# Sliding-window attention and a SMELU layer on one core: the first batch's q and k ahead of w_in, three SMELU slots on VectorE, and the last output tile in one piece

## The chip, the cores and the metric

The kernel runs on one core of a Trainium2 chip. The metric is the device time of one execution in microseconds. A profile, taken in one execution, shows what each engine did; its times count from the first instruction of its span.

## The reference

Eight batches with eight heads of 576 positions and 64 columns: attention in a window of 32 positions to each side, then a layer of 512 to 2048 to 512 columns with the SMELU function between its two products. All matrices come in float32, the output is float32.

```python
scores = scale * np.matmul(q, k.transpose(0, 1, 3, 2))
mask = np.abs(pos[:, None] - pos[None, :]) <= window        # window = 32
attn = softmax(np.where(mask, scores, -1e9))
x = (attn @ v).transpose(0, 2, 1, 3).reshape(4608, 512)
h = x @ w_in                                                # 512 x 2048
g = np.where(h >= 1, h, np.where(h <= -1, 0.0, (h + 1) ** 2 / 4))
out = g @ w_out                                             # 2048 x 512
```

## The kernel before

**Order.** All instructions stand in an order written out by hand; each engine runs its own in that order, and waits for what they read and for the buffers they write. A loop over `a` (line 483) runs through "slots". Slot a works on the 256 positions t = a // 8 and on 256 of the 2048 middle columns, f = a % 8. In a slot come: the products with w_in (eight matmuls, line 504, into the PSUM tile hp), SMELU, whose result goes to gT in bf16, then attention steps that the table `ev` puts there (`at(a, ...)`), then output products (`post`): the first four output tiles as "pairs" of 256 columns (function `pair`, line 460), all later ones as quarters of a tile (function `quarter`, line 444).

**SMELU.** ScalarE makes rr = relu(0.5 h + 0.5) (line 508). Then there are two ways: VectorE takes mx = max(h, rr) (line 515) and g = min(rr, 1) * mx (line 516); or, in the slots of the list `two_on_act`, ScalarE squares rr (line 512) and VectorE takes g = min(max(h, 1), rr²) (line 513). hp lies in a pool of two buffers (ps_h); slot 6 uses the pool ps_o.

**Attention.** For one batch, q and k are transposed on TensorE for batches 0 and 1 (`tpose`, line 187 and 189) and copied out of PSUM by ScalarE and VectorE (line 190); later batches are transposed by a DMA. `scores` adds a mask bias by matmul (line 206, early batches only), multiplies q and k (line 227) and takes exp on ScalarE (line 235); for later batches VectorE multiplies by a mask (line 201). `sums` multiplies by v and by ones (line 293) and has its quotient made as exp(-ln) on ScalarE (lines 299 and 300); VectorE's product with it is written to xT (lines 305 and 308), which is what slots read. `muls` and `flush` keep that last product back until VectorE's turn. The steps of `sums` and `scores` use the pools ps_s and ps_n, of one buffer each.

**Warm-up.** Ahead of slot 0, half of q and k of batch 0 is transposed and the first 256 positions of each pair of heads go through scores and sums. `keep_warm` puts matmuls without use in between (line 336). The other half (`qh`, `kh`, loaded by `load_half`, line 85) is transposed in slot 1, its scores follow in slots 2 and 3, its sums in slots 3 to 5.

**Loads.** All loads but q's first half are issued by GpSimd, with a cast to bf16, in the order of `put` (lines 144 to 157): v of batch 0, w_in for slots 0 and 1 (four loads of 128 KB, 64 rows of partitions each), the other half of q and k of batch 0 (four of 144 KB), w_in for slots 2 to 7 with w_out's first part among them, then three copies that build the masks (lines 151 and 153), w_out, and q, k and v of batch 1. Each load uses one of eight semaphores in turn, so each waits until the load eight places before it has landed. SyncE issues the stores and the DMA transposes.

**Tail.** The last output tile is made in two halves of 256 columns, and each is copied by ScalarE (line 437) and stored (line 438) by itself; a full tile is copied at line 449 and stored at line 450.

Of the kernel before, what the change touches and what calls it, by code (L numbers as in the profile page):

```python
# [7 lines left out]
FP = mybir.dt.float32  # L8
BF = mybir.dt.bfloat16
AF = mybir.ActivationFunctionType  # L10
ALU = mybir.AluOpType
# [3 lines left out]
def kernel(  # L15
# [19 lines left out]
    nc = tc.nc  # L35
# [106 lines left out]
    def put(todo):  # L142
        for fn, *x in todo:
            fn(*x)
# [1 line left out]
    w = [(load_w_in, c, c + 256, h) for c in range(0, 1024, 256) for h in range(2)]  # L146
    w += [(load_w_in, 1024, 1536, h) for h in range(2)]
    w += [(load_w_in, c, c + 256, h) for c in range(1536, DFF, 256) for h in range(2)]
    put(w[:4] + [(load_half, 1, t, h) for t in range(2) for h in range(2)] + w[4:12])
    put([(load_w_out, 0, 0, 4)] + w[12:])  # L150
    P.tensor_copy(band[HD[1], 0:128], band[HD[1], 64:192])
    for m, n, x in ((mask4, 8, 128), (mask8, 4, TAIL)):
        P.tensor_copy(m.rearrange("p (n j) -> p n j", n=n),
                      band[:, :x].rearrange("p (n j) -> p n j", n=1).to_broadcast([128, n, x]))
    put([(load_w_out, 0, 4, 8), (load_w_out, 0, 8, 16)] + [(load_rows, 1, t) for t in range(2)])
    put([(load_v, 1, n) for n in range(4)] + [(load_w_out, 1, 8 * n, 8 * n + 8) for n in range(2)])
    put([(load_nat, 2, t) for t in range(2)] + [(load_v, 2, n) for n in range(4)])

# [10 lines left out]
    def tpose(b, n, t, copy, ps):  # L169


        half, part = divmod(n, 2)
        j0, j1 = ((0, 5), (5, 9))[part]
        if b:
            src = qn[b] if t == 0 else kn[b]
            src = [src[:, half + 2 * h] for h in range(2)]
            dst = qkT(b, t).rearrange("d (y e p j) -> d y e p j", y=2, e=2, j=9)[:, half, :, :, j0:j1]
            like = "d j (e p) -> d e p j"
        else:
            src = (qn, kn)[t][b, half]  # L180
            src = src if src.shape[1] == 9 else [src[:, h] for h in range(2)]
            dst = qkT(b, t).rearrange("d (y l p j) -> d l y p j", l=2, p=32, j=9)[:, half, :, :, j0:j1]
            like = "d j (p y) -> d y p j"
        for j in range(j0, j1):
            if isinstance(src, list):
                for h in range(2):
                    nc.tensor.transpose(ps[HD[h], j - j0], src[h][:, D * j:D * j + D], ident)  # L187
            else:
                nc.tensor.transpose(ps[:, j - j0], src[:, j], ident)
        return lambda: copy(dst, ps[:, :j1 - j0].rearrange(like, p=64 if b else 32))  # L190
# [120 lines left out]
    def flush():  # L311
        while muls:
            muls.pop(0)()
# [18 lines left out]
    def keep_warm(n, pool, tag):  # L332

        z = pool.tile([128, 512], FP, name="z", tag=tag)
        for _ in range(n):
            nc.tensor.matmul(z, warm[:, :128], warm, start=True, stop=True)
# [9 lines left out]
    with tc.tile_pool(name="ps_p", bufs=1, space=bass.MemoryType.PSUM) as ps_p:  # L346
        keep_warm(11, ps_h, "hp")

        V.memset(qkT(0, 0).rearrange("d (y s) -> d y s", y=NY)[:, :, S // 2:352], 0.0)
        for b in range(LONG):  # L350
            V.memset(qkT(b, 0).rearrange("d (y s) -> d y s", y=NY)[:, :, S - PAD:], 0.0)
        V.memset(qkT(0, 1).rearrange("d (y s) -> d y s", y=NY)[:, :, S // 2:320], 0.0)
        qn[0, 0] = cast(q32, "qb", 5)
        qq = [tpose(0, n, 0, (A.copy, V.tensor_copy)[n], tp1(ps_h)) for n in range(2)]
        for x in qq:
            x()
        kk = [tpose(0, n, 1, (A.copy, V.tensor_copy)[n], tp1((ps_n, ps_p)[n])) for n in range(2)]
        keep_warm(3, ps_h, "hp")
        for x in kk:
            x()  # L360
        scores(0, (0, 1), (0, 2), (0, 2), None)
        scores(0, (0, 2), (0, 1), (2, 3), None, ps_n, 32)
        scores(0, (1, 2), (0, 2), (0, 2), None, ps_p)
        keep_warm(4, ps_h, "hp")
        e0 = sums(0, 0, 0, TB)
        keep_warm(2, ps_h, "hp")
        e1 = sums(0, 1, 0, TB, ps_p)
        keep_warm(7, ps_h, "hp")
        e0()
        e1()  # L370
    ps_o = ctx.enter_context(tc.tile_pool(name="ps_o", bufs=2, space=bass.MemoryType.PSUM))


# [1 line left out]

    NB = NT // TB
    NF = DFF // 256
    pairs = [(6, 0), (8, 1), (9, 2), (10, 3), (11, 4), (12, 5), (15, 6), (15, 8), (16, 7), (17, 9)]
    two_on_act = (1, 7, 8, 9, 10, 11, 12)
    ev = {}  # L380

    def at(a, *todo):


        ev.setdefault(a, []).extend(x for x in todo if x)
# [5 lines left out]
                yield (sums, b, y1, lo, hi), (scores, b, (y1, y1 + 1), (0, 2), (2 * k, 2 * k + 2))  # L391
        yield (sums, b, 0, MAIN, S), (scores8, b)

    at(1, (tposes, 0, (0, 1), (1, 1)))
    at(2, (scores, 0, (0, 1), (0, 2), (2, 4)), (scores8, 0, ps_o))
    at(3, (scores, 0, (1, 2), (0, 2), (2, 4), ps_n), (sums, 0, 0, TB, MAIN, ps_s))
    at(4, (sums, 0, 1, TB, MAIN))
    at(5, (sums, 0, 0, MAIN, S, ps_s))
    seq = [x for b in range(1, B) for x in steps(b, 224)]
    at(13, seq[0][1])  # L400
    at(13.5, (*seq[1][1], ps_n))
    at(14, (*seq[0][0], ps_s), seq[1][0])
    at(16, seq[2][1])
    for n, a in enumerate((18, 20, 26.5, 28)):
        at(a, seq[2 + n][0])
    for n, a in enumerate((18, 20, 26.5, 28)):
        at(a, seq[3 + n][1])
# [16 lines left out]
    def quarter(x):  # L424

        tt, ff = divmod(x, 4)
        if tt == NT // 128 - 1:
            half, n = divmod(ff, 2)
            if n == 0:
                op[tt] = ps_o.tile([128, 256], FP, name="op", tag="op")  # L430
            cols = slice(256 * half, 256 * half + 256)
            for j in range(NF * n, NF * n + NF):
                nc.tensor.matmul(op[tt], gT[tt // 2][:, j, 128 * (tt % 2):128 * (tt % 2) + 128], w_out[:, j, cols],  # L433
                                 start=j == 0, stop=j == 2 * NF - 1)
            if n:
                osb = osp.tile([128, 256], FP, name="osb")
                A.copy(osb, op[tt])
                nc.sync.dma_start(out=out[128 * tt:128 * tt + 128, cols], in_=osb)
            return
        if tt not in op:  # L440
            op[tt] = ps_o.tile([128, DM], FP, name="op", tag="op"), []
        o, done = op[tt]
        for j in range(4 * ff, 4 * ff + 4):
            nc.tensor.matmul(o, gT[tt // 2][:, j, 128 * (tt % 2):128 * (tt % 2) + 128], w_out[:, j],  # L444
                             start=not done, stop=len(done) == 2 * NF - 1, skip_group_check=True)
            done.append(j)
        if len(done) == 2 * NF:
            osb = osp.tile([128, DM], FP, name="osb")
            A.copy(osb, o)  # L449
            nc.sync.dma_start(out=out[128 * tt:128 * tt + 128, :], in_=osb)  # L450
# [31 lines left out]
    for a in range(NF * NB + NF):  # L482
        t, f = divmod(a, NF)
        eng = None if a < 14 else V
        post = [x for n, x in pairs if n == a] + [a - NF] * (a >= 2 * NF + 2)
        for b, x in loads.get(a, []):
            if x < 2:
                load_nat(b, x)
            else:
                for n in range(4):  # L490
                    load_v(b, n)
        if a == 0 or a > 3:
            flush()
        if t < NB:
            if t not in gT:
                gT[t] = gtp.tile([128, 2 * NF, TB], BF, name="gT", tag="gT")
            r0 = TB * t % RING
            if a == 6:
                hp = ps_o.tile([128, 2, TB], FP, name="hp", tag="op")
            else:  # L500
                hp = ps_h.tile([128, 2, TB], FP, name="hp", tag="hp")
            for j in range(2):
                for n, kk in enumerate((0, 2, 1, 3)):
                    nc.tensor.matmul(hp[:, j], w_in[:, kk, 256 * f + 128 * j:256 * f + 128 * j + 128],  # L504
                                     xT[:, kk, r0:r0 + TB], start=n == 0, stop=n == 3)

            rr = ewp.tile([128, 2, TB], FP, name="rr")
            A.activation(rr, hp, AF.Relu, scale=0.5, bias=0.5)  # L508
            g = gT[t][:, 2 * f:2 * f + 2]
            mx = ewp.tile([128, 2, TB], FP, name="mx")  # L510
            if a in two_on_act:
                A.activation(mx, rr, AF.Square)
                V.scalar_tensor_tensor(g, hp, 1.0, mx, op0=ALU.max, op1=ALU.min)
            else:
                V.tensor_max(mx, hp, rr)  # L515
                V.scalar_tensor_tensor(g, rr, 1.0, mx, op0=ALU.min, op1=ALU.mult)  # L516
        flush()
        run(a)
        for x in post:
            (pair if x < 4 * 4 else quarter)(x)  # L520
        run(a + 0.5)
        for x in xps.get(a, []):
            xpose(*x)
# [30 lines left out]
```

## Time and profile before

| | |
|---|---|
| median of 3 runs | 308.55 us (308.35 to 308.8) |
| the profiled execution's own time | 308.55 us |
| its span | 306.8 us |
| TensorE busy | 295.2 us, 96% of the span, 3613 matmuls |
| VectorE busy | 241.8 us, 79% |
| ScalarE busy | 192.3 us, 63% |
| GpSimd busy | 76.8 us, 25% |
| chain of waits, by engine | PE 88%, DMA 4%, issue 3%, ACT 2%, POOL 1%, DVE 1% |
| granted TensorE clock | 1.0 |

In the profile's lines PE is TensorE, PEld its weight loads, DVE VectorE, ACT ScalarE, POOL GpSimd, SP SyncE. L504 is line 504 of the kernel. A line of the timeline gives the start, the time, engine, line, operation, tiles and shape, the number of such operations, and in brackets the idle time of the engine before it and what ended it. The chain of waits is followed back from the last instruction: at each step to what released it.

### The profile page before, as it was taken

How to read it: one execution, taken by the hardware profiler on the slowest of the kernel's cores; microseconds unless marked ns; L12 is line 12 of the kernel's file. 1: busy time of each engine (PE TensorE's matmuls, PEld its weight loads, DVE VectorE, ACT ScalarE, POOL GpSimd, SP SyncE). 2: the span in 40 equal slices, each digit the busy share in tenths (PEclk: the TensorE clock that was granted, in tenths of full speed). 3: DMA queues.
4: the chain of work that ended last, by engine and by line, in shares of the span. 5: the costliest groups of instructions: out<-in, count | busy, mean ns of one | idle time of the engine just before them, and what ended most of it. 6: DMA issues, size and time to landing. Idle time of an engine off the chain costs nothing.

```text
span 306.8 us, 8458 instructions
## 1 busy us (share of the span) xinstructions
PE 295.2 (96%) x3613; PEld 206.8 (67%) x3650; DVE 241.8 (79%) x376; ACT 192.3 (63%) x320; POOL 76.8 (25%) x91
## 2 busy tenths in 40 slices
PE   8999999999999999999999999999999999999995
PEld 3567878876666666666666666666666666666654
DVE  4278568888888888889888888889888888888760
ACT  3688786738856667666656666566676666554431
POOL 8798451028008205500550002800000000000000
PEclk9999999999999999999999999999999999999999
DMA  9999999999999997996899155990811010010111
GB/s 150 182 196 197 179 201 151 175 153 151 133 208 82 171 164 124 155 114 141 103 168 140 34 112 105 142 158 17 178 49 36 34 36 36 35 36 34 61 44 68
DMA packets 137157, 35.70 MB, mean 116 GB/s; under 512 B 122144, under 2 KB 132896, under 8 KB 137120
## 3 DMA queue, kind: packets, MB, share of 16 engines
q0 software_dynamic: 102960, 18.06, 81.1%
q1 hardware_dynamic: 34016, 16.81, 25.6%
q8 instruction: 28, 0.46, 0.6%
q10 hardware_dynamic: 144, 0.29, 0.4%
q14 instruction: 9, 0.07, 0.1%
HBM read 36.70 MB, written 9.44 MB: 150 GB/s over the span
## 4 chain that ended last, share of the span: by engine, by line
PE 88%; DMA 4%; issue 3%; ACT 2%; POOL 1%; DVE 1%; POOLq 0%; ACTq 0%
PE hp L504 39%; PE op L444 34%; PE bb L293 6%; PE op L460 4%; PE bb L227 2%; DMA w_in<-in_moe_w_in_dram 2%; DMA vn<-in_v_dram 2%; PE op L433 1%; ACT pt L235 1%; PE tp L187 1%; POOL kh L85 1%; DVE xT L305 0%; DVE mx L515 0%; POOL vn L106 0%; PE bb L206 0%
## 5 line engine op out<-in xcount | busy, mean ns | idle before, releaser
L504 PE MATMUL hp<-xT,w_in 128*128 128x256 bf16 x1152 | 149.6, 273 | 1.4 <-DMA w_in<-in_moe_w_in_dram 0.6
L508 ACT ACTIVATE rr<-hp 128x512 f32<-128x512 f32 x144 | 85.6, 594 | 88.1 <-PE hp L504 88.1
L504 PEld LDWEIGHTS <-w_in 128*128 128x128 bf16 x1152 | 112.0, 98 | 41.1 <-issue 2.3
L444 PE MATMUL op<-w_out,gT 128*128 128x512 bf16 x461 | 119.6, 379 | 5.0 <-issue 4.8
L515 DVE TENSOR_TENSOR mx<-hp,rr 128x512 f32<-128x512 f32 x137 | 94.4, 689 | 30.9 <-ACT rr L508 28.9
L516 DVE SCALAR_TENSOR_TENSOR gT<-rr,mx 128x512 bf16<-128x512 f32 x137 | 95.2, 695 | 4.7
L444 PEld LDWEIGHTS <-gT 128*128 128x128 bf16 x496 | 46.1, 98 | 34.8
L98 POOL DMA_DIRECT2D qn<-in_q_dram x12 | 14.6, 1221 | 111.8 <-DMA kT<-kn 108.2
L235 ACT ACTIVATE pt<-bb 128x1024 bf16<-128x1024 f32 (+1 forms) x33 | 32.7, 1001 | 4.8 <-PE bb L227 3.4
L305 DVE TENSOR_TENSOR xT<-bb,rc 128x512 bf16<-128x512 f32 (+1 forms) x32 | 21.0, 657 | 10.1 <-ACT rc L300 9.5
L106 POOL DMA_DIRECT2D vn<-in_v_dram x32 | 27.5, 899 | 4.4 <-DMA w_out<-in_moe_w_out_dram 4.4
L300 ACT ACTIVATE rc<-lr 128x512 f32<-128x512 f32 (+2 forms) x40 | 23.5, 587 | 1.3
L449 ACT COPY osb<-op 128x512 f32<-128x512 f32 x31 | 18.0, 582 | 8.7 <-PE op L444 8.3
L299 ACT ACTIVATE lr<-bb 128x512 f32<-128x512 f32 (+2 forms) x40 | 22.1, 551 | 0.3 <-PE bb L293 0.3
L201 DVE TENSOR_TENSOR pt<-pt,mask 128x1024 bf16<-128x1024 bf16 (+1 forms) x33 | 20.2, 613 | 0.5 <-ACT pt L235 0.5
L293 PE MATMUL bb<-pt,ones 64*64 64x256 bf16 (+3 forms) x352 | 19.6, 256 | 0.1
L293 PE MATMUL bb<-pt,vn 64*64 64x128 bf16 (+3 forms) x712 | 18.4, 204 | 0.1
L293 PEld LDWEIGHTS <-vn 64*64 64x64 bf16 x712 | 16.7, 107 | 0.3 <-DMA vn<-in_v_dram 0.3
L460 PE MATMUL op<-w_out,gT 128*128 128x256 bf16 x128 | 16.5, 273 | 0.0
L293 PEld LDWEIGHTS <-ones 64*64 64x64 bf16 x352 | 10.2, 106 | 8.9 <-issue 8.9
L98 POOL DMA_DIRECT2D kn<-in_k_dram x12 | 14.6, 1231 | 0.7 <-issue 0.4
L460 PEld LDWEIGHTS <-gT 128*128 128x128 bf16 x128 | 12.0, 98 | 1.9
(59 smaller groups left out, 115.7 us busy)
## 6 DMA issues: line engine op xcount, KB each, us to landing
out_dram<-osb SPq DMA_DIRECT2D x35, 256.0 KB, 2.4
vn<-in_v_dram POOLq DMA_DIRECT2D x32, 144.0 KB, 10.5
qn<-in_q_dram POOLq DMA_DIRECT2D x12, 288.0 KB, 7.0
kn<-in_k_dram POOLq DMA_DIRECT2D x12, 288.0 KB, 9.3
w_in<-in_moe_w_in_dram POOLq DMA_DIRECT2D x12, 128.0 KB, 5.9
w_out<-in_moe_w_out_dram POOLq DMA_DIRECT2D x3, 512.0 KB, 15.2
kh<-in_k_dram POOLq DMA_DIRECT2D x4, 144.0 KB, 5.2
qn<-in_q_dram POOLq DMA_DIRECT2D x1, 576.0 KB, 9.5
```

The lines of the kernel that those rows point to most:

```text
L98: nc.gpsimd.dma_start(out=x[:, :, h], in_=src[b, NY * h:NY * h + NY].rearrange("y s d -> (y s) d") .rearrange("(u p) d -> p u d", p=128))
L106: nc.gpsimd.dma_start(out=vn[b][64 * a:64 * a + 64, :, h], in_=v[b, y:y + 2].rearrange("y s d -> (y s) d") .rearrange("(c r) d -> r c d", ...
L235: A.activation(p, ps[:, :, :w * n].rearrange(like, y=m), AF.Exp, scale=D ** -0.5)
L293: nc.tensor.matmul(bb[HD[h], a, o + c0:o + c1], ones[HD[a]] if c is None else vn[b][HD[a], c, h], p(a, h), start=n == 0, stop=True, skip_g ...
L299: A.activation(lr[:, :, :D0], bb[:, :, D0:2 * D0], AF.Ln)
L300: A.activation(rc[:, :, :D0], lr[:, :, :D0], AF.Exp, scale=-1.0)
L444: nc.tensor.matmul(o, gT[tt // 2][:, j, 128 * (tt % 2):128 * (tt % 2) + 128], w_out[:, j], start=not done, stop=len(done) == 2 * NF - 1, s ...
L460: nc.tensor.matmul(o[:, tt], gT[p][:, j, 128 * tt:128 * tt + 128], w_out[:, j, 256 * half:256 * half + 256], start=not done, stop=len(done ...
L504: nc.tensor.matmul(hp[:, j], w_in[:, kk, 256 * f + 128 * j:256 * f + 128 * j + 128], xT[:, kk, r0:r0 + TB], start=n == 0, stop=n == 3)
L508: A.activation(rr, hp, AF.Relu, scale=0.5, bias=0.5)
L515: V.tensor_max(mx, hp, rr)
L516: V.scalar_tensor_tensor(g, rr, 1.0, mx, op0=ALU.min, op1=ALU.mult)
```

## The change

Five things change. The other half of q and k of batch 0 is loaded ahead of all of w_in, and the three mask copies are issued after the loads of q and k of batch 1. That half is transposed in the warm-up, q's copies on VectorE, k's on ScalarE, with the warm matmuls there cut from 7 to 2; its scores move to slots 0 and 1, its sums to slots 2 to 4. SMELU in slots 0 to 2 is made by VectorE alone, in three operations; slots 3 and 4 (for 6) use the pool ps_o for hp, and the list `two_on_act` loses 1 and 7 and gains 4 and 6. Pairs 0, 2, 3, 4 and 5 move by one slot, one score step of batch 1 from 13 to 13.5, one sums step from 26.5 to 22. The last output tile is made like all others.

```diff
-    put(w[:4] + [(load_half, 1, t, h) for t in range(2) for h in range(2)] + w[4:12])
-    put([(load_w_out, 0, 0, 4)] + w[12:])
+    put([(load_half, 1, t, h) for t in range(2) for h in range(2)] + w)
+    put([(load_w_out, 0, 0, 4), (load_w_out, 0, 4, 8), (load_w_out, 0, 8, 16)] + [(load_rows, 1, t) for t in range(2)])
     P.tensor_copy(band[HD[1], 0:128], band[HD[1], 64:192])
     for m, n, x in ((mask4, 8, 128), (mask8, 4, TAIL)):
         P.tensor_copy(m.rearrange("p (n j) -> p n j", n=n),
                       band[:, :x].rearrange("p (n j) -> p n j", n=1).to_broadcast([128, n, x]))
-    put([(load_w_out, 0, 4, 8), (load_w_out, 0, 8, 16)] + [(load_rows, 1, t) for t in range(2)])
...
         e1 = sums(0, 1, 0, TB, ps_p)
-        keep_warm(7, ps_h, "hp")
+        tp = [pool.tile([128, 2, 8, 128], BF, name="tp", tag="bb") for pool in (ps_s, ps_n)]
         e0()
+        flush()
+        c = [tpose(0, 2 + n, 0, V.tensor_copy, tp[0][:, n]) for n in range(2)]
+        c[0]()
         e1()
+        flush()
+        c[1]()
+        for x in [tpose(0, 2 + n, 1, A.copy, tp[1][:, n]) for n in range(2)]:
+            x()
+        keep_warm(2, ps_h, "hp")
...
-    pairs = [(6, 0), (8, 1), (9, 2), (10, 3), (11, 4), (12, 5), (15, 6), (15, 8), (16, 7), (17, 9)]
-    two_on_act = (1, 7, 8, 9, 10, 11, 12)
+    pairs = [(7, 0), (8, 1), (10, 2), (11, 3), (12, 4), (13, 5), (15, 6), (15, 8), (16, 7), (17, 9)]
+    on_dve = (0, 1, 2)
+    two_on_act = (4, 6, 8, 9, 10, 11, 12)
...
-    at(1, (tposes, 0, (0, 1), (1, 1)))
-    at(2, (scores, 0, (0, 1), (0, 2), (2, 4)), (scores8, 0, ps_o))
-    at(3, (scores, 0, (1, 2), (0, 2), (2, 4), ps_n), (sums, 0, 0, TB, MAIN, ps_s))
-    at(4, (sums, 0, 1, TB, MAIN))
-    at(5, (sums, 0, 0, MAIN, S, ps_s))
+    at(0, (scores, 0, (0, 1), (0, 2), (2, 4)))
+    at(1, (scores8, 0, ps_o), (scores, 0, (1, 2), (0, 2), (2, 4), ps_n))
+    at(2, (sums, 0, 0, TB, MAIN, ps_s))
+    at(3, (sums, 0, 1, TB, MAIN))
+    at(4, (sums, 0, 0, MAIN, S, ps_s))
...
-    at(13, seq[0][1])
-    at(13.5, (*seq[1][1], ps_n))
+    at(13.5, seq[0][1], (*seq[1][1], ps_n))
...
-    for n, a in enumerate((18, 20, 26.5, 28)):
+    for n, a in enumerate((18, 20, 22, 28)):
         at(a, seq[2 + n][0])
...
     def quarter(x):
         tt, ff = divmod(x, 4)
-        if tt == NT // 128 - 1:
...
-                osb = osp.tile([128, 256], FP, name="osb")
-                A.copy(osb, op[tt])
-                nc.sync.dma_start(out=out[128 * tt:128 * tt + 128, cols], in_=osb)
-            return
...
-        if a == 0 or a > 3:
-            flush()
+        flush()
...
-            if a == 6:
+            if a in (3, 4):
                 hp = ps_o.tile([128, 2, TB], FP, name="hp", tag="op")
...
-            A.activation(rr, hp, AF.Relu, scale=0.5, bias=0.5)
+            if a not in on_dve:
+                A.activation(rr, hp, AF.Relu, scale=0.5, bias=0.5)
             g = gT[t][:, 2 * f:2 * f + 2]
             mx = ewp.tile([128, 2, TB], FP, name="mx")
-            if a in two_on_act:
+            if a in on_dve:
+                V.tensor_scalar(rr, hp, -1.0, 1.0, op0=ALU.max, op1=ALU.add)
+                V.scalar_tensor_tensor(mx, rr, 0.25, rr, op0=ALU.mult, op1=ALU.mult)
+                V.scalar_tensor_tensor(g, hp, 1.0, mx, op0=ALU.max, op1=ALU.min)
+            elif a in two_on_act:
```

More of the change, by code (lines that the diff above doesn't have):

```diff
@@ L426, in quarter @@
         tt, ff = divmod(x, 4)
-        if tt == NT // 128 - 1:
[L428 to L435, printed above, removed]
-                osb = osp.tile([128, 256], FP, name="osb")
-                A.copy(osb, op[tt])
-                nc.sync.dma_start(out=out[128 * tt:128 * tt + 128, cols], in_=osb)
-            return
         if tt not in op:
```

## The prediction, as it was put on record

> **What bounds the kernel now.** I read the busy times by stage first, then the chain of waits, then single engines in the stages that the diff touches. Columns of the first view: stretch, length, busy time of PE, PEld, DVE, ACT, POOL, granted clock, share of the DMA engines, GB/s.
>
> ```profile
> 0.00:13.79 13.79, 12.30 (x160) 6.04 (x163) 4.43 (x17) 7.89 (x11) 11.73 (x22) 1.00 1.49 162
> 13.79:28.42 14.63, 13.19 (x245) 9.97 (x244) 11.51 (x18) 11.12 (x22) 13.54 (x19) 1.00 1.38 197
> 28.42:44.17 15.75, 15.58 (x256) 12.75 (x256) 9.33 (x15) 13.30 (x22) 8.54 (x9) 1.00 1.72 192
> 44.17:299.70 255.53, 250.51 (x2929) 174.98 (x2957) 216.54 (x328) 158.66 (x265) 42.95 (x42) 1.00 1.02 106
> ```
>
> From 44.17 us on TensorE is never held up: matmuls follow each other at 0.11 us (256 columns) or 0.22 us (512), and no step between two is longer than a lost record explains. The diff leaves that work as it is. So only the front (to 44.17) and the tail (from 299.70) can change. The chain of waits, in order of time (start, us, what), says what sets the front:
>
> ```profile
> 12.19 5.94 DMA w_in<-in_moe_w_in_dram
> 18.27 1.03 PE hp L504 x8
> ...
> 27.82 0.56 DVE xT L308
> 28.38 0.04 issue
> 28.42 1.03 PE hp L504 x8
> 29.46 0.87 PE op L460 x8
> ```
>
> A transfer holds slot 2's matmuls to 18.27; then ScalarE and VectorE alternate until VectorE's last xT write releases slot 8 at 28.42; from there it is TensorE. The loads are a stream of about 197 GB/s that never pauses, and they land in the order of issue. Issue times plus time to landing give: w_in of slot 0 at 11.25 and 11.91, of slot 1 at 12.63 and 14.44, then the rest of q at 14.72 and 15.32, of k at 16.14 and 16.94, w_in of slot 2 at 17.44 and 18.13, of slot 3 at 18.82 and 19.53, of slots 4 and 5 at 20.77 and 22.12. Slot 4 starts at 22.26: it is on that stream too.
>
> **Part 1, the loads.** Four q/k loads (144 KB each) change places with four w_in loads (128 KB). Everything from slot 2's w_in on has the same bytes ahead of it, so 18.13, 19.53 and 22.12 stay. The swapped ones take the places of the others, later by 0.07 us for each bigger load (16 KB at 197 GB/s is 0.08): q about 11.3 and 12.0, k about 12.8 and 14.6 (14.44 and most of the growth), slot 0's w_in about 14.9 and 15.5, slot 1's 16.8. The step from 12.63 to 14.44, against 0.6 to 0.8 elsewhere, I keep in place: it hits whatever lands fourth.
>
> **Part 2, the start of slot 0.** In before its matmuls start at 13.79 and go on at 14.60. After, the k transposes stand ahead of it: 14.6, 0.04 to react (16.94 to 16.98 in before), 0.47 for the transposes (16.98 to 17.45), 0.15 to the next matmul, two warm matmuls at 0.22: **15.70**. Slot 0's w_in is there at 15.5. The five dropped warm matmuls and the moved transposes lie in TensorE's wait and cost nothing; if the loads came earlier they would. The copies of q (VectorE, up to 0.85 each) end by 15.4, those of k (ScalarE, 0.76) by 16.4, ahead of scores at 16.7: hidden.
>
> **Part 3, VectorE.** How its operations follow each other (start, duration):
>
> ```profile
> 24.09 0.62 DVE L305 TENSOR_TENSOR xT<-bb,rc 128x448 bf16<-128x448 f32 x1 [0.55 <-ACT rc L300]
> 24.64 0.68 DVE L515 TENSOR_TENSOR mx<-hp,rr 128x512 f32<-128x512 f32 x1
> 25.35 0.69 DVE L516 SCALAR_TENSOR_TENSOR gT<-rr,mx 128x512 bf16<-128x512 f32 x1
> 25.96 0.62 DVE L305 TENSOR_TENSOR xT<-bb,rc 128x448 bf16<-128x448 f32 x1
> 26.49 0.68 DVE L515 TENSOR_TENSOR mx<-hp,rr 128x512 f32<-128x512 f32 x1
> ...
> 27.82 0.55 DVE L308 TENSOR_TENSOR xT<-bb,rc 128x384 bf16<-128x384 f32 x1
> 28.29 0.68 DVE L515 TENSOR_TENSOR mx<-hp,rr 128x512 f32<-128x512 f32 x1
> ```
>
> An operation that reads the one before starts 0.71 to 0.72 after it, an independent one 0.61, one behind an xT write 0.55 (tail: 0.47). Slots 0 to 2 each get three chained operations. The first two have no row here. The nearest of that shape and type are L515 and L516, 0.69; from below, the bf16 mask product of 384 elements takes 0.35; from above, the widened 1.10 shown further down. I take 0.69, so a slot is 0.72+0.72+0.61=2.05, with ends 1.4 and 2.9.
>
> VectorE starts on slot 0 when its matmuls end, 15.70+1.05=16.75, and from then on each next input is ready before VectorE is: slot 1's matmuls end at 18.4 (needed 18.8), slot 2's, which wait for slot 0's third operation, at 20.1 (20.85), ScalarE's rr of slot 5 comes at 26.2 (26.4). So VectorE runs without a break: three slots 6.15, xT 0.55, slot 3 1.32, xT 0.55, slot 4 0.61, tail xT 0.47, slot 5's first operation 0.68, in all 10.33, to 27.08. That operation frees the buffer (two in the pool, slots 3 and 4 use the other pool) in which **slot 7** writes; TensorE, done with slot 6 at about 25.8, waits until 27.11. Pair 0 now comes behind slot 7, so slot 8 starts at 27.11+2×0.87=28.85. In before it started at 28.42, with the same slots, transposes and pair 0 behind it: **+0.43**. The transposes' 1.2 us that left TensorE's queue, and the stall of 0.6 ahead of slot 2, are gained, but TensorE spends them waiting for VectorE.
>
> **Part 4, from slot 8 to slot 15.** No pair is left at slot 9, so slot 10 follows slot 9 at once, and its buffer is slot 8's: matmuls to 29.89, rr and square on ScalarE 0.63+0.66, product on VectorE 0.69, 31.89, while TensorE is free at 28.85+3×0.87=31.46. That is 0.43 against a wait of 0.18 in before (slot 9): +0.25. At slot 13 pair 5 stands ahead of the scores, so the wait of 0.22 for the copies of k there goes: −0.25 with what follows. Other moved events (tail sums from 26.5 to 22) lie where nothing waits; if that were wrong, I'd expect 0.1 to 0.3. Front: **+0.43**.
>
> **Part 5, the tail.**
>
> ```profile
> 299.90 0.58 ACT L449 COPY osb<-op 128x512 f32<-128x512 f32 x1 [2.87 <-PE op L444]
> 301.65 0.37 ACT L437 COPY osb<-op 128x256 f32<-128x256 f32 x1 [1.16 <-PE op L433]
> 302.05 2.12 SPq L438 DMA_DIRECT2D out_dram<-osb  x2
> 303.44 0.37 ACT L437 COPY osb<-op 128x256 f32<-128x256 f32 x1 [1.42 <-PE op L433]
> ```
>
> TensorE ends as before (16×0.2165 for 32×0.1085). The last copy takes 0.58 for 0.37 (+0.21) and the last store, by the row of 300.51, 2.00 to landing for 1.71 (+0.29); the copy follows a little closer (−0.05): **+0.45**. Nothing is beside it.
>
> **Sum.** The profiled execution took 308.55 (span 306.8 and 1.75 around it), which is also the median. 308.55+0.43+0.45=**309.4**.
>
> **Rivals.**
> VectorE collides with the masks (slower). In before one operation that reads two SBUF tiles ran 1.10 instead of 0.69, beside GpSimd's mask copies:
>
> ```profile
> 20.69 1.10 DVE L516 SCALAR_TENSOR_TENSOR gT<-rr,mx 128x512 bf16<-128x512 f32 x1
> ```
>
> The masks stood at 20.21 to 22.16, where VectorE had slack. After, they come behind the k load of batch 1, at about 24.15 to 26.1, and slot 3's gT, of that kind, is due at 24.17, in the chain that sets slot 7: +0.41, 309.8. Against it: which starts first is open. The Trainium skill (SBUF — State Buffer, SBUF: two separate sides) says the shared port pair is held for the whole instruction, and a VectorE operation with two SBUF inputs is blocked by a GpSimd one that reads SBUF; by it the wait could be the long copy's whole length, up to some 1.4 us, and the total 310.8. The row shows 0.41.
>
> The late fourth load is an accident (not slower). If the step to 14.44 is no part of the stream, k lands at 13.6 and slot 0's w_in at 14.95: slot 0 starts at 15.15, VectorE's chain moves by −0.55, and the total is 308.9. It decides from a landing of k before 14.1 on. For it: nothing in the diff makes that step; against: TensorE's program up to it is unchanged, and nothing says that it moves.
>
> TensorE sets the front (faster). If the buffer of slot 5 came free by 25.25, slot 4 (held to 22.2 by its load), tail sums 0.45, slots 5 and 6, slot 7 and pair 0 give slot 8 at 27.0, −1.4; q of batch 1 (33.2 in before) then holds its transposes some 0.3, so −1.1+0.45: 307.9. It needs three slots at the lower price of 1.4 instead of 2.05, and rr of slot 5 a microsecond earlier than ScalarE's queue (rr, square, lr, rc, rr behind slot 4) allows.
>
> TensorE's pause before the k transposes, about 1.4 us, is longer than before's 0.6, and its first warm matmuls ran at 0.43 us instead of 0.22. The Trainium skill (TensorE: Matmul & The Clock Gate, What's actually happening) has the clock halved after an idle window of about 3.4 us; by it this pause costs nothing.
>
> **Chances.** Forecast 0.43; masks 0.23; late load 0.22; TensorE 0.12. A difference under 0.2% (0.62 us) can hardly be told from none. The forecast lies 0.23 above that bound with some 0.4 of doubt, so about a third of it counts as same, as do most of the third case and a third of the fourth; slower takes two thirds of the first and nearly all of the second: slower 0.55, same 0.33, faster 0.12. The range leaves out the TensorE case and the long mask wait: 308.2 to 310.6.
>
> **What would show it.** Slot 0's matmuls at 15.7; VectorE without a gap from 16.75 to 28.4 and three operations of about 0.69 in slots 0 to 2; TensorE waiting 1 us or more for VectorE ahead of slot 7; slot 15 at 44.6 instead of 44.17; the last copy 0.58 and the last store 2.0. A gap in VectorE's row ahead of slot 7, or slot 8 before 28.0, would prove the sum wrong.

## The result, and the profile after

The changed kernel takes 310.28 us in the median of 6 runs (309.79 to 311.33), the kernel before 308.61 us in 6 runs beside them (308.35 to 309.11). The ratio is 1.0056, with a 95% interval of 1.0039 to 1.0074: slower by about 1.7 us. The profiled execution took 309.79 us, span 308.0, against 308.55 and 306.8 before: 1.24 us more. The prediction's time, 309.4, lies between the two medians, and its range, 308.2 to 310.6, holds the result.

The busy times by stage after the change; the stages are cut at the same places of the work (start of slot 0, of slot 8, of slot 15, start of the last output tile). Columns: stretch, length, busy time of PE, PEld, DVE, ACT, POOL, granted clock, share of the DMA engines, GB/s.

```profile
0.00:15.62 15.62, 12.38 (x192) 6.41 (x194) 6.56 (x20) 8.32 (x12) 12.57 (x24) 1.00 1.45 168
15.62:28.80 13.18, 11.46 (x210) 8.97 (x209) 11.40 (x19) 10.46 (x19) 11.50 (x17) 1.00 1.39 192
28.80:44.67 15.87, 15.34 (x258) 12.71 (x256) 8.83 (x14) 12.22 (x20) 9.36 (x11) 1.00 1.73 194
44.67:300.42 255.75, 250.74 (x2929) 174.94 (x2957) 216.69 (x328) 158.87 (x265) 42.95 (x42) 1.00 1.02 105
```

The first two stages together are 0.38 us longer than before (28.80 against 28.42): slot 0 starts 1.83 us later, and slots 0 to 7 take 1.45 us less. The third is 15.87 for 15.75. The fourth, which the prediction left alone, is 255.75 for 255.53: 0.22 us that it did not have.

The chain of waits after the change, from the load that slot 4 waits for (start, us, what; short pieces called issue are left out here and in the chains below):

```profile
16.00 6.39 DMA w_in<-in_moe_w_in_dram
...
22.53 1.05 PE hp L497 x8
23.60 0.61 ACT rr L502
...
25.24 0.67 DVE gT L511
25.92 0.46 DVE xT L307
26.38 0.63 DVE mx L513
27.05 1.03 PE hp L497 x8
28.09 0.87 PE op L454 x8
```

Slot 7 starts at 27.05, as forecast (27.11), and VectorE's product mx is what releases it, as forecast too. But the chain does not come from VectorE's slots 0 to 2. It comes from a load: w_in of slots 4 and 5 lands at 22.39, slot 4's matmuls follow, and 4.52 us after their start slot 7 begins. VectorE's own chain is just as long:

```profile
16.69 0.69 DVE L506 TENSOR_SCALAR rr<-hp 128x512 f32<-128x512 f32 x1 [1.37 <-PE hp L497]
17.42 0.69 DVE L507 SCALAR_TENSOR_TENSOR mx<-rr 128x512 f32<-128x512 f32 x1
18.15 0.69 DVE L508 SCALAR_TENSOR_TENSOR gT<-hp,mx 128x512 bf16<-128x512 f32 x1
18.75 0.68 DVE L506 TENSOR_SCALAR rr<-hp 128x512 f32<-128x512 f32 x1
```

Starts of 16.69, 17.42, 18.15 and 18.75: a slot is 2.06 us, and there is no idle time in brackets until 28.75. From 16.69 to slot 7 it is 10.35 us with the reaction, so this chain ends at 27.04. Two chains end together, and the profile names the one that came last by 0.01.

Behind slot 8 one line is new. Slot 9 has no pair now, so slot 10 follows it at once and waits for slot 8's SMELU, two operations on ScalarE and one on VectorE:

```profile
29.93 0.61 ACT rr L502
30.56 0.64 ACT mx L510
31.22 0.70 DVE gT L511
31.97 1.03 PE hp L497 x8
```

Slot 9 starts at 30.54 and its eight matmuls take 0.87, so slot 10 waits 0.56 us.

### The profile page after: what moved, and what is told of

It is laid out like the page before. It is cut to its first block, busy times and chain, and to the rows that moved or that the text cites. A ratio compares the mean times of both kernels' runs of the same rounds, so it can differ in the third digit from the quotient of the medians.

```text
span 308.0 us, 8412 instructions
## 1 busy us (share of the span) xinstructions
PE 293.5 (95%) x3591; PEld 204.5 (66%) x3629; DVE 243.5 (79%) x379; ACT 191.0 (62%) x316; POOL 76.4 (25%) x91
## 4 chain that ended last, share of the span: by engine, by line
PE 87%; DMA 4%; POOL 2%; issue 2%; ACT 2%; DVE 1%; POOLq 0%; ACTq 0%
PE hp L497 39%; PE op L438 35%; PE bb L292 6%; PE op L454 4%; DMA kh<-in_k_dram 2%; DMA w_in<-in_moe_w_in_dram 2%; PE bb L226 2%; POOL vn L106 1%; PE tp L186 1%; ACT pt L234 1%; POOL kh L85 0%; DVE gT L511 0%; ACT rr L502 0%; POOL w_in L110 0%; POOL qh L85 0%
## 5 line engine op out<-in xcount | busy, mean ns | idle before, releaser
L502 ACT ACTIVATE rr<-hp 128x512 f32<-128x512 f32 x141 | 83.7, 594 | 86.8 <-PE hp L497 85.3
L438 PE MATMUL op<-w_out,gT 128*128 128x512 bf16 x476 | 122.8, 379 | 5.1 <-issue 4.8
L513 DVE TENSOR_TENSOR mx<-hp,rr 128x512 f32<-128x512 f32 x134 | 92.4, 689 | 30.5 <-ACT rr L502 28.3
L514 DVE SCALAR_TENSOR_TENSOR gT<-rr,mx 128x512 bf16<-128x512 f32 x134 | 92.7, 692 | 4.6
L438 PEld LDWEIGHTS <-gT 128*128 128x128 bf16 x512 | 47.6, 98 | 36.7
L98 POOL DMA_DIRECT2D qn<-in_q_dram x12 | 14.6, 1224 | 113.1 <-DMA kT<-kn 109.0
L200 DVE TENSOR_TENSOR pt<-pt,mask 128x1024 bf16<-128x1024 bf16 (+1 forms) x33 | 20.2, 613 | 0.2 <-ACT pt L234 0.2
L98 POOL DMA_DIRECT2D kn<-in_k_dram x12 | 14.6, 1235 | 0.3
L454 PEld LDWEIGHTS <-gT 128*128 128x128 bf16 x128 | 12.0, 98 | 1.9
```

The costliest lines, as they stand in the source:

```text
L98: nc.gpsimd.dma_start(out=x[:, :, h], in_=src[b, NY * h:NY * h + NY].rearrange("y s d -> (y s) d") .rearrange("(u p) d -> p u d", p=128))
L454: nc.tensor.matmul(o[:, tt], gT[p][:, j, 128 * tt:128 * tt + 128], w_out[:, j, 256 * half:256 * half + 256], start=not done, stop=len(done ...
```

## The experiments

Some names stand in the expectations. The theory of the first four kernels is the prediction's sum with the missed step that the fourth stage shows. N says that slot 7 waits for the later of two chains: VectorE's start plus 10.35, and slot 4's start plus 4.52. Its rival V says that VectorE's chain alone sets it, its rival L that the load alone does. The changed kernel was timed in six runs only, and its ratio is known to 0.18% on either side, so medians of two kernels that differ by 0.3 us say little; for such sizes the offsets between traces are read. All runs of the kernel before, beside which the others were timed, have medians of 308.61 to 308.89 us.

**e1: the sums step back at 26.5.**

```diff
-    for n, a in enumerate((18, 20, 22, 28)):
+    for n, a in enumerate((18, 20, 26.5, 28)):
```

> The changed kernel with the last sums step of batch 1 put back from slot 22 to 26.5. Theory (a step that stands alone costs TensorE two more changes between full-array and 64-row matmuls, +0.22 from slot 21 to slot 27 in the profile): 0.2 us below the changed kernel, so about 309.6 in the profiled execution's terms and 310.05 for the median; slot 27 starts 0.50 after before's instead of 0.72. Rival (the step is free, the 0.22 is the front's still working through): no change, 310.3.

309.75 us, ratio 1.0031 (1.0018 to 1.0045); 310.05 was expected. The profiled execution took 310.34, because slot 4's load landed 0.80 us later in it than in the changed kernel's (23.19 for 22.39). So slot 15 starts 1.30 us later than before, and slot 27 1.29: the offset no longer grows, which is where the theory and its rival differ. In the changed kernel it grows from 0.50 to 0.72 between slots 21 and 27. From slot 15 to the last slot it is 250.34 us before and in e1, 250.56 in the changed kernel and in e2. The changed kernel's timeline of TensorE shows the step by itself:

```profile
60.92 0.28 PE L292 MATMUL bb<-pt,ones 64*64 64x192 bf16 x4
...
61.20 0.20 PE L292 MATMUL bb<-pt,vn 64*64 64x64 bf16 x4
61.34 1.05 PE L454 MATMUL op<-w_out,gT 128*128 128x256 bf16 x8
```

In before these matmuls on 64x64 tiles stood directly ahead of a score step's, also on 64x64 tiles, and shared with it the way into that tiling and the way out:

```profile
68.54 0.20 PE L293 MATMUL bb<-pt,vn 64*64 64x64 bf16 x4
68.57 0.40 PE L227 MATMUL bb<-qT,kT 64*64 64x128 bf16 x16
```

Alone, the step pays for both again: 0.20 us from the last 128x128 matmul's start to its first, 0.13 from its last to the next 128x128 one, less the 0.11 that these two would have needed anyway. The Trainium skill (TensorEngine Tiling (Array Packing), Tiling Modes) says that a change of the tiling mode drains TensorE; in this trace one more visit costs 0.22 us.

**e2: the last tile in two halves again** (the branch that the change took out of `quarter`, put back).

> The changed kernel with the last output tile made in two column halves again. Theory (tail +0.45: last copy 0.58 for 0.37, last store 2.0 for 1.7): 0.4 to 0.45 below the changed kernel, 309.85; the span from the last matmul to the end is before's. Rival (the change's loss lies elsewhere, the whole tile costs nothing because fewer matmuls and weight loads make up for it): no change, 310.3.

309.73 us, ratio 1.003 (1.002 to 1.004). The tail's price is the forecast's: in the changed kernel the last copy and the last store behind it are

```profile
304.07 0.58 ACT L443 COPY osb<-op 128x512 f32<-128x512 f32 x1 [2.87 <-PE op L438]
```

0.58 for 0.37, and 2.01 from issue to landing for 1.71. The last store lands 11.47 us after the last slot's start in the changed kernel, 11.04 before and 11.03 in e2: +0.43, and e2 takes it back. The median fell by 0.55, which agrees within what the six runs allow.

**e3: six warm matmuls in TensorE's pause ahead of the k transposes.**

```diff
         c = [tpose(0, 2 + n, 0, V.tensor_copy, tp[0][:, n]) for n in range(2)]
+        keep_warm(6, ps_h, "hp")
```

> The changed kernel with six more warm matmuls between the transposes of q and of k, in TensorE's pause of 1.1 us. Theory (the pause lets the granted clock drop in some executions, which would be why the other runs of the changed kernel are 0.3 to 1.5 us above the profiled one): median 309.8 and a spread like before's, clock 1.0 in every run. Rival (the pause does nothing to the clock; the spread is of the loads): 310.3 with the same spread and the same clocks of 0.997 to 1.0.

310.11 us, ratio 1.0043 (1.0029 to 1.0056), from 309.89 to 310.28 in 5 runs. The spread is narrow as the theory had it, but the median hardly lower, and the clocks are 0.997 to 1.0 as the rival had them: inconclusive by itself.

**e4: the old SMELU in slots 0 to 2.**

```diff
-    on_dve = (0, 1, 2)
-    two_on_act = (4, 6, 8, 9, 10, 11, 12)
+    on_dve = ()
+    two_on_act = (1, 4, 6, 8, 9, 10, 11, 12)
```

> The changed kernel with SMELU of slots 0 to 2 made as in before (ScalarE first, slot 1 with the square on ScalarE). Theory (VectorE's chain of 10.3 us from slot 0 sets slot 7; without three operations it would be 2.1 shorter, but slot 4's load at 22.2 and ScalarE's queue behind it hold slot 7 to about 26.8): slot 7 0.3 to 0.5 earlier, median 309.9. Rival A (VectorE alone is the bound, nothing close behind it): slot 7 at 25.3, median 308.6. Rival B (ScalarE, now with four more operations ahead of slot 3, becomes the bound): slower than the changed kernel, 310.6 or more.

310.6 us, ratio 1.0055 (1.004 to 1.007): no gain, where 309.9 was expected. VectorE now has two operations or one in each of these slots for three, and slot 7 starts at 28.23. In this execution slot 4's load landed at 23.57, its matmuls started at 23.71, and 4.52 later comes 28.23. This was the first sign of the second chain. The median alone doesn't tell it from rival B, which had 310.6 too; b1, below, which has this edit without the late load, shows that ScalarE's queue costs something as well: 0.22 us from slot 0 to slot 7 against b2.

**e5: the load order alone**, put into the kernel before.

```diff
-    put(w[:4] + [(load_half, 1, t, h) for t in range(2) for h in range(2)] + w[4:12])
+    put([(load_half, 1, t, h) for t in range(2) for h in range(2)] + w[:12])
```

> The kernel before with one part of the change: the rest of q and k of batch 0 loaded ahead of all w_in, w_in following in order; nothing else. Theory: slot 0 goes from 13.8 to 15.5 (its w_in lands third and fourth later), slot 1 to 16.9, slot 2 to about 18.9 instead of 18.27, and ScalarE's and VectorE's queue behind it moves with it: +0.5 us, 309.3. Rival (slots 2 to 4 are held by their own loads, which do not move): below +0.2.

310.68 us, ratio 1.0055 (1.0035 to 1.0075): as slow as the whole change, where 0.5 us was expected. Its chain of waits:

```profile
17.30 1.05 PE hp L504 x8
...
19.67 0.69 DVE gT L513
20.36 0.69 DVE qT L190
21.04 0.65 DVE kT L190
21.73 0.45 PE bb L227 x16
```

Slots 0 and 1 start late (15.91 and 17.30), and the transposes, which this kernel still makes in slot 1, have their copies behind slot 1's SMELU on VectorE; scores, sums and slot 8 follow late, slot 8 at 30.48 for 28.42. The changed kernel, which transposes in the warm-up, has slot 8 at 28.80. So the load order, put alone into the kernel before, costs 2.06 us at slot 8, and the rest of the change gives 1.68 of it back.

**e7: two operations for three** in slots 0 to 2 of the changed kernel. The middle one, the square, is left out.

```diff
-                V.scalar_tensor_tensor(mx, rr, 0.25, rr, op0=ALU.mult, op1=ALU.mult)
-                V.scalar_tensor_tensor(g, hp, 1.0, mx, op0=ALU.max, op1=ALU.min)
+                V.scalar_tensor_tensor(g, hp, 1.0, rr, op0=ALU.max, op1=ALU.min)
```

> The changed kernel with the second of VectorE's three operations left out in slots 0 to 2, so that SMELU there is a clipped line without its square (the output is not the reference's; the time is read for the chain alone). VectorE's chain from slot 0 to slot 7 gets 2.1 us shorter. Theory N (two chains of nearly equal length set slot 7: VectorE's, 10.35 after slot 0's matmuls end, and that of slot 4's load, whose matmuls are followed by slot 7 after 4.52): slot 7 stays 4.5 behind slot 4, near 27.0; median within 0.2 of the changed kernel's, 310.1 to 310.3. Rival V (my step as put on record: VectorE's chain is the bound): slot 7 near 25.3, median 308.6 to 309.0.

310.18 us, ratio 1.0041 (1.0027 to 1.0054). Some 2.1 us are taken from VectorE's chain and the median gains next to nothing: V falls, which had 308.6 to 309.0. That the load holds slot 7 instead this trace doesn't show: slot 4's load landed at 23.15, but TensorE got to slot 4 only at 23.71. This execution (311.12, the slowest of its eight) ran late for another reason, seen in the busy times of three stretches:

```profile
11.64:15.05 3.41, 1.85 (x57) 1.30 (x57) 2.39 (x4) 2.18 (x4) 1.90 (x4) 1.00 1.35 197
15.05:18.46 3.41, 3.41 (x31) 1.90 (x29) 0.26 (x1) 1.35 (x2) 3.40 (x6) 0.50 1.44 195
18.46:21.87 3.41, 3.41 (x81) 2.47 (x84) 2.86 (x5) 2.50 (x4) 2.87 (x5) 1.00 1.23 182
```

From 15.05 to 18.46 the granted clock is 0.50, and TensorE makes 31 matmuls where it makes 81 afterwards.

**e8: the load of slots 4 and 5 in two**, slot 4's part first.

```diff
-    w += [(load_w_in, 1024, 1536, h) for h in range(2)]
+    w += [(load_w_in, c, c + 256, h) for c in (1024, 1280) for h in range(2)]
```

> The changed kernel with the 512-column loads of w_in for slots 4 and 5 cut in two each, slot 4's first. Slot 4's load then has 256 KB less ahead of it and lands 1.3 earlier in the worst order, 21.1 to 21.5. Theory N: slot 4 at 22.1 (behind slot 3 and its sums), slot 7 held by VectorE's chain at 27.05 to 27.2; the profiled execution gains 0.1 at most, but executions with a late load (slot 4 at 23.3 or 23.7) go, so the median falls by 0.3, to 310.0, and the highest run below 310.5. Rival L (the load is the bound alone): slot 7 at 26.6, median 309.6. Rival V: no change in median or spread.

309.93 us, ratio 1.0031 (1.0018 to 1.0044), 309.39 to 311.49 in 12 runs. Slot 4's load lands at 21.43. Its chain of waits now comes through VectorE without a break, from 17.21 to slot 7 at 27.56, which is 10.35. Slot 7 is later here than in the changed kernel because slot 0 is: it starts at 16.14 for 15.62, 0.13 after its own w_in, which landed at 16.01 for 15.42. From slot 0 to slot 7 it is 11.42 us in e8 and 11.43 in the changed kernel, so with the load early VectorE's chain holds slot 7 just as long, and L falls. The median fell about as N had it (310.0), though by less than the runs can resolve; that the slowest run stayed at 311.49 is not as N had it.

**e9: e7 and e8 together**.

> Both edits at once: the loads cut in two, and the second VectorE operation of slots 0 to 2 left out (output not the reference's). Theory N: each alone gives little, both together free slot 7: slot 4 at 22.1, slot 7 near 26.6 (ScalarE's queue behind slot 4 is next), 0.45 below the changed kernel in the profile and 0.7 in the median, 309.6. Rival V: the same as without the cut, about 308.8. Rival L: the same as with the cut alone.

309.48 us, ratio 1.0021 (1.0005 to 1.0037). Both chains shortened, slot 7 starts at 26.81, which is 10.96 after slot 0 for 11.43. In the medians both edits take 0.8 us, where e7 takes 0.1 and e8 0.35 (the step from e8 to e9 is not clear of noise in the medians; the offset from slot 0 shows it). That is what two chains of one length look like. And a third ends last here, soon behind them, from the sums of slot 2 through ScalarE's quotients and VectorE's xT:

```profile
20.79 0.56 ACT lr L298
21.36 0.59 ACT rc L299
21.98 0.62 DVE xT L304
...
24.52 0.48 ACT lr L298
25.03 0.53 ACT rc L299
25.59 0.56 DVE xT L307
26.14 0.63 DVE mx L512
26.81 1.03 PE hp L497 x8
```

The same in all traces of these kernels, b1 and b2 from below among them (times in us; VectorE's start is its first operation on hp; the bound that decides in bold, where it is one of the two):

| kernel | slot 4 starts, +4.52 | VectorE starts, +10.35 | slot 7 starts |
|---|---|---|---|
| changed | 22.53, **27.05** | 16.69, 27.04 | 27.05 |
| e1 | 23.32, **27.84** | 16.89, 27.24 | 27.85 |
| e2 | 22.68, **27.20** | 16.83, 27.18 | 27.20 |
| e3 | 22.49, 27.01 | 16.85, **27.20** | 27.18 |
| e4 | 23.71, **28.23** | another chain | 28.23 |
| e8 | 22.51, 27.03 | 17.21, **27.56** | 27.56 |
| b2 | 22.04, 26.56 | 16.74, **27.09** | 27.09 |
| e7 | 23.71, 28.23 | three operations fewer | 28.41, third chain |
| e9 | 22.11, 26.63 | three operations fewer | 26.81, third chain |
| b1 | 22.20, 26.72 | another chain | 27.57, ScalarE's queue |

**b1 and b2: the changed kernel with what the runs above suggest.** Both have e1, e2, e3 and e8 together, and the pairs 2 to 4 back at slots 9 to 11; b1 has e4 as well.

```diff
-    pairs = [(7, 0), (8, 1), (10, 2), (11, 3), (12, 4), (13, 5), (15, 6), (15, 8), (16, 7), (17, 9)]
+    pairs = [(7, 0), (8, 1), (9, 2), (10, 3), (11, 4), (13, 5), (15, 6), (15, 8), (16, 7), (17, 9)]
```

> After with five edits: the load of w_in for slots 4 and 5 cut in two with slot 4's part first, the last tile in halves, the sums step back at 26.5, pairs 2 to 4 back at slots 9 to 11, six warm matmuls in TensorE's pause, and the old SMELU of slots 0 to 2 (rr on ScalarE). Theory N (slot 7 waits for the later of two chains, VectorE's and slot 4's load): with the load at 21.4 VectorE's chain is the bound, and with it short too slot 7 starts 0.7 us earlier than in b2; I expect 0.4 below b2, some 308.5. Rival (the other order: VectorE alone is no dearer, since slot 1's rr then waits on ScalarE behind the copies of k): b1 within 0.2 of b2.

> As b1, but slots 0 to 2 keep SMELU on VectorE alone. Sum of the single measurements: 310.3 less 0.45 (halves), 0.2 (sums step), 0.35 (split load) and 0.2 (warm matmuls and pairs), 309.0. Rival (the parts share one wait and their gains don't add up): 309.5.

b2: 308.95 us (308.78 to 309.15 in 12 runs), ratio 0.9998 (0.9988 to 1.0007): level with the kernel before, and as its sum had it. b1: 309.22 us (308.67 to 309.42), ratio 1.0004 (0.9994 to 1.0015). The expectation for b1, 308.5, had the wrong sign: with the load out of the way VectorE's SMELU is no cost, it is worth some 0.3 us (eight of b1's twelve runs lie above b2's slowest). Its chain of waits comes through ScalarE's queue:

```profile
22.60 0.58 ACT rr L516
...
25.27 0.48 ACT lr L298
25.78 0.53 ACT rc L299
26.33 0.56 DVE xT L307
26.89 0.63 DVE mx L527
27.57 1.03 PE hp L511 x8
```

With rr of slots 0 to 2 back on ScalarE, which from 17.01 on has no break, the quotient of the last sums step is late, VectorE waits for it, and slot 7 starts at 27.57; in b2, where VectorE makes all of these slots, at 27.09. Part of these 0.48 us is b1's later start (slot 0 at 15.93 for 15.67). And from slot 8 to slot 15 both take 15.58 us, where the changed kernel takes 15.87 and before 15.75: the pairs back at slots 9 to 11 remove the wait of 0.56 at slot 10, and with no pair at slot 12 one of 0.28 behind slot 13 comes back.

**b3: the kernel before with two edits**, the split load of e8, and pair 5 at slot 13 with both score steps of batch 1 at 13.5.

> Before with two edits: the load of slots 4 and 5 cut in two, slot 4's first, and pair 5 at slot 13 with its score step at 13.5 (the one move of the change that took a wait away). Theory N: slot 4 starts some 0.7 earlier, but in before VectorE's queue sets slot 8, so little of it comes through; the wait of 0.22 at slot 13 goes: 0.25 below before, 308.6. Rival (the load sets before's front too): 0.7 below, 308.2.

309.24 us, ratio 1.0013 (1.0001 to 1.0025): slower by 0.4 us instead of faster. Slot 4's load lands 1.1 us earlier, but slot 4 doesn't start 0.7 earlier, as N had it: TensorE gets there at 22.24 for 22.26. Slot 8 starts at 28.52 for 28.42. In the profiled execution the loss comes behind it:

```profile
32.67 1.03 PE L459 MATMUL op<-w_out,gT 128*128 128x256 bf16 x8 [1.16 <-DMA w_out<-in_moe_w_out_dram]
```

The two more transfers put off the mask copies on GpSimd, and behind them the last parts of w_out: the last is issued 1.08 us later (23.93 for 22.85). They land at 29.56 and 32.62 for 27.51 and 30.45; the second half of that delay is not explained. Pair 2 at slot 9 waits 1.16 us for them. (This execution took 310.0, the longest of b3's twelve; the median's share of that wait is smaller.) In the changed kernel and in b2 these loads are issued ahead of the mask copies and have landed by 30.85. Moving pair 5 gave nothing: the offset to before is 1.45 at slot 10 and at slot 15. Between the transposes of k in slot 12 and the scores there is one pair here, as in before; the changed kernel has two there, pairs 4 and 5. From slot 13 to slot 14, less a pair where there is one, it is 2.23 us before, 2.25 in b3 and b2, and 1.97 in the changed kernel: the wait goes by the second pair, not by pair 5's place.

**b4: b3 with the opposite of the change's load order**, slot 2's w_in ahead of the other half of q and k.

```diff
-    put(w[:4] + [(load_half, 1, t, h) for t in range(2) for h in range(2)] + w[4:12])
+    put(w[:6] + [(load_half, 1, t, h) for t in range(2) for h in range(2)] + w[6:12])
-    at(1, (tposes, 0, (0, 1), (1, 1)))
-    at(2, (scores, 0, (0, 1), (0, 2), (2, 4)), (scores8, 0, ps_o))
-    at(3, (scores, 0, (1, 2), (0, 2), (2, 4), ps_n), (sums, 0, 0, TB, MAIN, ps_s))
-    at(4, (sums, 0, 1, TB, MAIN))
+    at(2, (tposes, 0, (0, 1), (1, 1)))
+    at(3, (scores, 0, (0, 1), (0, 2), (2, 4)), (scores8, 0, ps_o), (scores, 0, (1, 2), (0, 2), (2, 4), ps_n))
+    at(4, (sums, 0, 0, TB, MAIN, ps_s))
+    at(4.5, (sums, 0, 1, TB, MAIN))
```

> b3 with the opposite of the change's load order: slot 2's w_in ahead of the other half of q and k, whose transposes move to slot 2 and scores to slot 3. The stall ahead of slot 2 in before (0.6 us for its load) goes, and VectorE begins its slots earlier: 0.3 to 0.9 below before, some 308.0 to 308.6. Rival (the scores and sums that come a slot later hold slot 8, which reads their xT): as b3 or up to 0.5 slower.

310.4 us, ratio 1.0046 (1.0033 to 1.0059): slower, as the rival had it, but by more, and by a wait that comes earlier than the rival's at slot 8. Slot 3 starts 0.48 us earlier than before, slot 6 1.56 later: VectorE stands idle 1.38 us for ScalarE's rr, which is queued behind the exponentials of three score steps in one slot. The order of before lies between two that are dearer, as far as these two show it.

No kernel of the study beats the one before.

## Why the prediction was right, and where it was not

The range held the result; the number, +0.85 us, is half of the +1.67 that the medians show. The profiled executions differ by 1.24 us, of which the traces give 1.15:

| term | forecast | measured |
|---|---|---|
| slot 8 (VectorE's chain, slot 7, pair 0) | +0.43 | +0.38 (28.80 for 28.42) |
| slot 8 to slot 15 (Part 4) | +0.25 − 0.25 | +0.12 (+0.38 at slot 10, where 0.56 is waited for 0.18 at slot 9; −0.26 behind slot 13) |
| sums step moved to 22 | 0 (0.1 to 0.3 if wrong) | +0.22 |
| tail | +0.45 | +0.43 |

- **Loads and slot 0 (Parts 1 and 2): right.** k lands at 14.51 (14.6 forecast), slot 0's w_in at 14.88 and 15.42 (14.9 and 15.5), slot 0 starts at 15.62 (15.70). The late fourth load stayed where it was, on another transfer, so the second rival did not occur (in e8 the third load is the late one, at 14.55). But k and slot 0's w_in lie close together: in e1, e2 and e8 w_in lands at 15.63 to 16.01 and slot 0 starts 0.13 behind it. One landing of Part 1 was off, slot 4's, said to stay at 22.12.
- **VectorE (Part 3): the sizes right, the claim that it sets slot 7 alone wrong.** Three operations of 0.69, 2.06 a slot, 10.35 to slot 7. Part 3 took for granted that "each next input is ready before VectorE is", and had slot 4's rr by the load's old time. With the load at 22.12 that would have held with 0.26 us to spare (22.26 + 4.52 = 26.78); it landed at 22.39 in the profiled execution, and at 22.35 to 23.57 in the others with the uncut load. e4 and e7 shorten VectorE's chain and gain nothing, e9 shortens both and gains, the table above has each. All the signs that the prediction named for itself came true, slot 0 at 15.7, VectorE without a gap, the wait ahead of slot 7: none of them could tell one chain from two.
- **Slot 8 to slot 15 (Part 4): both terms there, the first too small.** Slot 10 starts 3.17 us after slot 8, where the sum had 3.04. The −0.25 is −0.26, by one more pair between the transposes of k and the scores.
- **Moved events "lie where nothing waits": wrong.** Nothing waits there, but TensorE is the bound there, so two more changes of tiling count in full. The price was inside the 0.1 to 0.3 given for that case.
- **The tail: right,** nothing covers it.
- **The rivals.** The masks' copies came after slot 3's gT had started, and it was the first copy that was held: it took 0.36 us for 0.29 and ended 0.15 behind gT.

```profile
24.09 0.69 DVE L514 SCALAR_TENSOR_TENSOR gT<-rr,mx 128x512 bf16<-128x512 f32 x1
24.57 0.36 POOL L151 COPY band<-band 64x128 bf16<-64x128 bf16 x1
```

  The other two copies (24.99 to 26.48) met no operation on two SBUF tiles. Where such a copy starts first, gT is held: 0.83 us in b3 and 0.97 in b4, as 1.10 in before.

```profile
21.53 1.95 POOL L153 COPY mask<-band 128x1024 bf16<-128x1024 bf16 x2
22.14 0.97 DVE L515 SCALAR_TENSOR_TENSOR gT<-rr,mx 128x512 bf16<-128x512 f32 x1
```

  (These are b4's.) The long copy by itself takes 1.04 us, so the prediction's 1.4 for a wait of its whole length was too much. TensorE as the bound of the front did not occur.
- **The median above the profiled run (+0.43 of the 1.67).** The forecast added profiled differences to the median. The changed kernel's six runs spread over 1.5 us, the six of before over 0.8. Three things that differ from execution to execution are shown: the landing of slot 4's load, which after the change lies on a chain without slack; slot 0's start, from which VectorE's chain counts, 15.62 in the changed kernel's trace and up to 16.14 in the others at full clock; and the half clock of e7, though none of the changed kernel's six runs has a mean clock under 0.997. How much each adds to its median is not shown. b2, which has the load early and the pause filled, spreads over 0.37 us in 12 runs. Which of its two edits narrows it was not separated: e3 has only the filled pause and spreads over 0.39 in 5 runs, e8 only the split load and over 2.1 us in 12.
- **The clock.** The profiled run of the changed kernel has a clock of 1.0 throughout, so the pause before the k transposes cost nothing there. In e7 a pause cost something, as far as one event shows. The Trainium skill (TensorE: Matmul & The Clock Gate, What's actually happening) has the clock halved after an idle window of about 3.4 us, and has these windows run free of the kernel; the prediction took from it that a pause of 1.4 us is safe. In e7 the clock rises to full at 4.81 us and falls at 15.05, three times 3.41 later. The window ahead, from 11.64 to 15.05, was not idle: TensorE was busy for 1.85 of 3.41 us in it, with no gap over 1.20, and the next 3.41 us ran at half clock. Windows counted in the same way held 1.98 busy us in the changed kernel (from 12.17), 1.96 in e5 and 1.90 in e9, and the clock stayed. So the measurement corrects the reading: a window about half empty can be enough. That the place of the windows decides is likely, but with one event not shown.

What stays open is why slot 4's load lands at different times. One candidate is on the profile's list of DMA queues: packets of 16 KB that it calls instruction. In the stretch from 20.2 to 21.3 us of the changed kernel, while that load is under way, there is one:

```profile
q0 software_dynamic: 260, 0.19, 121.3%
q8 instruction: 1, 0.02, 5.1%
```

5.1% of 16 engines for 1.1 us is 0.9 us on one DMA engine. The second half of slot 4's load lands 1.61 us after the first here and 1.57 to 2.56 in the other kernels with the uncut load; in before it is 1.35, and there the packet came at 21.93 and the load behind, slot 6's, has the long step (22.83 to 24.03). Against it: in e8 such a packet, at 19.87, goes with no late landing. No experiment moved a packet, so this is argued, not shown.

## What to carry to other kernels

When a chain is worked out to be the bound, work out the next one too, with the slack between them: here two ended within 0.01 us and a third within half a microsecond, so shortening any one gave little or nothing. A step moved on the engine that sets the time is not free because nothing waits for it; ask what it shared with its old neighbours. And a load order that favours one consumer is paid by all that stand behind it in the same stream, w_out behind a GpSimd copy included.

## What the runs showed of the hardware that was not expected

- A TensorE clock of 0.50 for 3.41 us after a stretch of 3.41 us in which TensorE was busy 54% of the time (e7). Mean clocks of 0.993 to 0.994 in two runs of e5, one of e7 and one of e9 fit the same event (half of 3.41 us in 309 is 0.55%); they took 0.6 to 2.1 us longer than their kernel's median.
- One extra visit to 64x64 tiles between 128x128 matmuls: 0.22 us.
- Of a VectorE operation on two SBUF tiles and a GpSimd copy in SBUF that overlap, the one that starts later was held, in each of the traces read for it: gT took 0.83 to 1.10 us for 0.69 (before, b3, b4), the small copy 0.36 and 0.51 for 0.29 (changed kernel, e8).
- Cutting a load in two, with the same bytes, went with a landing of w_out's last part 2.2 us later in the profiled execution (b3); 1.1 us of it is the later issue, as more transfers stand ahead of the mask copies that GpSimd makes in between.
